# Two transformer layers on one core: weighted V copies kept per layer, a six-tile ring for the residual stream, and two score banks read by one VectorE instruction

## The chip, the cores and the metric

The kernel runs on one core of a Trainium2 chip. The metric is the device time of one execution in microseconds; lower is better. The kernel before takes 1658.69 us, the median of 3 runs (1657.44 to 1659.52). A core has five engines that run their own instruction streams and wait for each other through semaphores: TensorE (PE, matmuls into PSUM), ScalarE (ACT), VectorE (DVE), GpSimd (POOL) and SyncE (SP), which here issues all DMA transfers. PSUM has eight banks, each 128 partitions by 512 f32 numbers.

## The reference, cut to what matters

Four steps on x of shape [1, 2048, 512] in bf16: attention, MLP, attention, MLP, with the same weights in both rounds. The kernel calls the two attention steps layer 1 and layer 3.

```python
def _A_ref(x, wqkv, wo):            # attention, 32 heads of 16
    B, S, D = x.shape
    H = 32; Dh = D // H
    qkv = (x @ wqkv).reshape(B, S, 3, H, Dh).transpose(2, 0, 3, 1, 4)
    q, k, v = qkv[0], qkv[1], qkv[2]
    scores = jnp.einsum("bhqd,bhkd->bhqk", q, k) * Dh ** -0.5
    p = softmax(scores, axis=-1)
    o = jnp.einsum("bhqk,bhkd->bhqd", p, v)
    return o.transpose(0, 2, 1, 3).reshape(B, S, D) @ wo

def _B_ref(x, w1, b1, w2, b2):      # MLP, 512 -> 1376 -> 512
    y = layernorm(x)
    h = gelu(y @ w1 + b1)           # tanh form
    return h @ w2 + b2

x = A_x
x = x + _A_ref(layernorm(x), A_wqkv, A_wo)
x = x + _B_ref(layernorm(x), B_w1, B_b1, B_w2, B_b2)
x = x + _A_ref(layernorm(x), A_wqkv, A_wo)
x = x + _B_ref(layernorm(x), B_w1, B_b1, B_w2, B_b2)
```

## The kernel before

The Python program is a scheduler: it simulates the five engines with an estimated duration for every instruction, picks for each engine the ready task of lowest priority number, and writes out five fixed instruction streams. The durations in the code (0.66, 0.1 + 0.26e-3 * N and so on) are these estimates; on the chip only the order and the semaphore waits remain.

Attention goes by segments: one group of four heads (hg), one chunk of 512 queries (qc), 16 blocks of 128 keys (kb). A tile is one block of keys against 512 queries for one head (hp): a 128x512 matmul result in one PSUM bank. Most tiles are exponentiated by ScalarE, three and two banks in turn:

```python
            if self.wide:
                b0, G = ((0, 3), (3, 2))[gi % 2]
            ...
            S_.submit(Task("act", 1e-5 * gi, [I(lambda e, pt=pt, n=n, b0=b0: e.activation(out=self.PT[:, pt:pt + n, :], in_=self.ps[:, b0:b0 + n, :], func=ACTF.Exp, scale=EXPS), ...
```

Tiles of the key blocks DK = (3, 6, 9, 12, 15) may go to VectorE, which builds the bit pattern of the exponential by adding a constant to the scores and storing 16-bit integers. One such approximation is rough, so four of them are averaged, each shifted by a constant (SHIFT) and multiplied by a V that is scaled to match (WSHIFT). A tile on VectorE therefore costs one load from PSUM, shifts for k = 1, 2, 3 (two tiles in one instruction), and four matmuls with V instead of one:

```python
SHIFT = (0, 32, 64, 96)
WSHIFT = (1.0, 0.83984375, 0.70703125, 0.59375)
DK = (3, 6, 9, 12, 15)

    def d_load(self, d):                       # one score bank -> one half of dp[u]
        sg, j, b, bt, w = d
        ...
        self.S_.submit(Task("dve", 0.0, [I(lambda e: e.tensor_scalar(out=self.dp[:, u, w * 512:(w + 1) * 512], in0=self.ps[:, b, :], scalar1=BITS0, scalar2=None, op0=ALU.add), ...

    def job_d(self, bt):                       # the three shifts of a batch of two tiles
        for k in range(1, len(SHIFT)):
            v = yield ("get", "dp", sg["i"])
            pr = 0.15 if ... else 0.5 if self.left(sg) < DURGE else 2.5
            yield Task("dve", pr, [I(lambda e, k=k, v=v: e.tensor_scalar(out=self.dp[:, v, 0:N], in0=self.dp[:, u, 0:N], scalar1=float(SHIFT[k]), ...
```

Which tile goes where is decided while the program is written: `take_d` gives VectorE a tile only if one of two banks is free (the lane bank 5, or bank 7, MISCB, which projections and FFN also use), if VectorE is not behind, and if the scaled V is there. What is left over goes to ScalarE:

```python
    grp.append((sg, (sg["todo"] or sg["todod"]).pop(0)))      # ScalarE takes DK tiles when no others are left

    def take_d(self, hps):
        if ... self.dload > 1 or P.free["dve"] - S_.now > 1.3 or ... > DBACK:
            return None
        if not self.lane_busy and ("ret", DLANE) in S_.done and soon(DLANE):
            b = DLANE
        elif MISCB in mb.free and not mb.waiters and soon(MISCB):
            b = MISCB
        else:
            return None
        ...
        if not all(k in self.S_.done for k in [("qt", sg["i"])] + self.kv_keys(sg, kbs) + [("vs", sg["i"], kb) for kb in kbs]):
            return None
```

The scaled copies of V are made by GpSimd anew for every segment, three instructions each, into one of three slots:

```python
        self.vs = t("vs", [128, 3, 3, len(DK), 68], BF16)

    def job_vs(self, sg, i, kbs):
        q, hg, n = sg["qslot"], sg["hg"], len(kbs)
        src = self.V[:, hg, kbs[0]:kbs[-1] + 1:3, :, :].rearrange("p k h d -> p k (h d)")
        yield Task("pool", 0.8, [I(lambda e, k=k: e.tensor_scalar(out=self.vs[:, q, k - 1, i:i + n, :], in0=src, scalar1=WSHIFT[k], ...) for k in (1, 2, 3)])
```

Probabilities times V are summed in one PSUM bank (ACCB, bank 6), four heads side by side in the columns of the array. When a chunk of queries is done, the projection, layer norm and MLP of that chunk (`job_post`, `job_ffn`) run between the tiles of the next chunk; then its keys, values and queries for layer 3 are made. The residual stream is kept whole on the chip:

```python
        self.xres = t("xres", [128, NT, 512], BF16)           # NT = 16 tiles
        ...
            S_.submit(Task("dve", pr - 1, [I(lambda e, tt=tt, b=b: e.tensor_tensor(out=self.xres[:, tt, :], in0=self.ps[:, b, :], in1=self.xres[:, tt, :], op=ALU.add), ...
```

In gaps TensorE multiplies a zero tile (`fill_pe`)[...].

Of the kernel before, what the change touches and what calls it, by code (L numbers as in the profile page):

```python
# [8 lines left out]
BF16 = mybir.dt.bfloat16  # L9
# [4 lines left out]
ACTF = mybir.ActivationFunctionType  # L14
# [420 lines left out]
D_PRIO = 0.5  # L435
DBATCH = 2
DFLY = 4
# [3 lines left out]
ACCB = 6  # L441
MISCB = 7
DTAIL = 8
DURGE = 8
PV_NEAR = 0.7
PV_DEEP = 2
PV_COST = 0.5
PV_LEAST = 0.75
PV_IDLE = 0.25


class Builder:
# [44 lines left out]
    def alloc(self, es):  # L497
# [3 lines left out]
        self.xres = t("xres", [128, NT, 512], BF16)  # L501
# [27 lines left out]
        self.vs = t("vs", [128, 3, 3, len(DK), 68], BF16)  # L529
# [28 lines left out]
        self.q_scr = nc.dram_tensor("q_scr", [2, S, 1024], BF16, kind="Internal").ap()  # L558
        self.k_scr = nc.dram_tensor("k_scr", [S, 1024], BF16, kind="Internal").ap()
# [5 lines left out]
        pl["mb"] = Pool([7, 5, 4, 3, 2, 1, 0])  # L565
# [15 lines left out]
        pl["kmx"] = Pool(range(1))  # L581

# [39 lines left out]
    def build_startup(self):  # L622
# [5 lines left out]
        def ldx(a, b):  # L628
            n0("sp", I(lambda e: e.dma_start(self.xres[:, a:b, :], xr[:, a:b, :]), writes=[("x", tt) for tt in range(a, b)], dur=0.1))
# [9 lines left out]
        self.S_.when([("ks", 1, 1)], lambda: ldx(4, 8))  # L639
# [127 lines left out]
    def ln_group(self, tiles, slot, prio, eps1, eps0):  # L767

        for i, tt in enumerate(tiles):
            c = 4 * slot + i  # L770
            s = yield ("get", "st")
            yield Task("dve", prio, [I(lambda e, s=s, tt=tt: e.bn_stats(out=self.st[:, s, :], in_=self.xres[:, tt, :]), [("x", tt)], [("st", s)], 0.65)])
# [10 lines left out]
    def ln_apply(self, tt, slot, i, dst, dres, prio):  # L783
        c = 4 * slot + i
        return Task("dve", prio, [I(lambda e: e.tensor_scalar(out=dst, in0=self.xres[:, tt, :], scalar1=self.mv[:, c, 0:1], scalar2=self.rs[:, c:c + 1], op0=ALU.subtract, op1=ALU.mult),
                                    [("x", tt), ("mv", c), ("rs", slot)], [dres], 0.39)])
# [4 lines left out]
    def job_lnqkv(self, L, tiles, prio, later=None):  # L791
# [9 lines left out]
        if later is not None:  # L801
            yield ("keys", [("n2k", L, tt) for tt in range(self.NT)])
            for i, tt in enumerate(tiles):
                self.S_.spawn(self.job_qkv_tile(L, tt, slot, i, left, later + 0.01 * i, "q"), later + 0.01 * i)

    def job_qkv_tile(self, L, tt, slot, i, left, prio, what):
# [4 lines left out]
        yield self.ln_apply(tt, slot, i, xnr, RX, prio)  # L811
        left[0] -= 1
# [42 lines left out]
        if "v" in what:  # L855
# [3 lines left out]
            if direct:  # L859
# [3 lines left out]
                yield Task("dve", prio, [I(lambda e: e.tensor_copy(out=vdst, in_=psv), [("ps", b)], VR, 0.68)])  # L863
                S_.when([("ks", L, tt)], lambda: S_.mark(("kv", L, tt)))
# [849 lines left out]
```

## Time and profile before

The profile is one execution, recorded by the hardware profiler, with a span of 1661.8 us. What matters for the change:

| group (line of the kernel) | engine | instructions | busy us | mean ns |
|---|---|---|---|---|
| exponentials of score tiles, 1189 | ScalarE | 1321 | 1506.4 | 1259 with table loads |
| score matmuls, 1204 | TensorE | 4608 | 681.8 | 359 |
| loads of score tiles, 1281 | VectorE | 826 | 558.2 | 684 |
| shifts, 1312 | VectorE | 1257 | 488.8 | 431 |
| scaled V copies, 1065 | GpSimd | 240 | 238.5 | 995 |
| matmuls on a zero tile, 1114 | TensorE | 3792 | 182.0 | 277 |
| additions to the residual stream, 1469 and 1540 | VectorE | 60 | 40.9 | 682 |

Busy time counts each stretch in which a group has an instruction running once. The mean is of the single instructions; they overlap a little, so the mean times the count is more than the busy time. Matmuls overlap much more, and their ends are modelled, so a busy TensorE is not one at its limit. GpSimd's idle time before the scaled copies is 875.3 us. The mean traffic is 40 GB/s, and packets on the main DMA queue take 17.3% of the time of the 16 engines.

### The profile page before, as it was taken

The page shows a single profiled execution, that of the slowest core. Times are in us where ns is not written, and L with a number is a line of the kernel's source. Part 1 is how long each engine was busy: PE and PEld are TensorE (multiplying, and loading weights), DVE is VectorE, ACT ScalarE, POOL GpSimd, SP SyncE. Part 2 cuts the span into 40 slices and gives each one's busy share as a digit, 9 for nine tenths or more (in the row PEclk, how much of TensorE's full clock was granted, in tenths as well). Part 3 has the DMA queues.
Part 4 walks back from the last instruction along what each step waited for, and adds up shares of the span by engine and source line. Part 5 has one row for each costly group of instructions (what it writes and reads, how often), then busy time and mean ns, then how long its engine had stood idle before and what let it go on. Part 6 is the DMA issues. An engine that isn't in the chain of part 4 may idle for free.

```text
span 1661.8 us, 42068 instructions
## 1 busy us (share of the span) xinstructions
PE 1608.0 (97%) x17575; PEld 529.0 (32%) x17575; DVE 1452.7 (87%) x3146; ACT 1582.4 (95%) x1400; POOL 376.1 (23%) x575
## 2 busy tenths in 40 slices
PE   8999999999999999999999999999999999999998
PEld 5223322222222232222232323322232232344444
DVE  7789998888899898998989789999898969899893
ACT  4899999999999999999999999999999999999996
POOL 4345331111210112111121125511111111232220
PEclk9999999999999999999999999999999999899999
DMA  6562100202111121102362321000000000000000
GB/s 170 103 125 62 27 8 8 42 19 61 56 23 42 26 52 53 33 26 58 95 94 57 59 64 42 18 18 8 20 5 11 17 16 5 5 9 20 22 7 14
DMA packets 181243, 66.43 MB, mean 40 GB/s; under 512 B 160859, under 2 KB 175424, under 8 KB 181056
## 3 DMA queue, kind: packets, MB, share of 16 engines
q1 hardware_dynamic: 181056, 63.75, 17.3%
q8 instruction: 141, 2.31, 0.6%
q14 instruction: 46, 0.38, 0.1%
HBM read 19.96 MB, written 15.30 MB: 21 GB/s over the span
## 4 chain that ended last, share of the span: by engine, by line
PE 65%; ACT 27%; DVE 6%; issue 1%; DMA 1%; POOL 0%; POOLq 0%; SPq 0%; DVEq 0%
ACT PT L1189 25%; PE ps L1204 24%; PE ps L1373 19%; PE ps L840 5%; PE ps L1500 4%; PE ps L1538 4%; PE ps L1114 4%; PE ps L1467 3%; DVE dp L1281 2%; DVE dp L1312 2%; ACT h L1530 1%; PE ps L1117 1%; PE ps L953 1%; DMA xnT<-xn 0%; ACT L1189 0%
## 5 line engine op out<-in xcount | busy, mean ns | idle before, releaser
L1189 ACT ACTIVATE PT<-ps 128x1024 bf16<-128x1024 f32 (+1 forms) x1321 | 1506.4, 1259 | 49.5 <-PE ps L1204 43.1
L1204 PE MATMUL ps<-QT,KT 32*128 32x512 bf16 (+1 forms) x4608 | 681.8, 359 | 39.0 <-ACT PT L1189 16.9
L1281 DVE TENSOR_SCALAR dp<-ps 128x512 uint16<-128x512 f32 x826 | 558.2, 684 | 117.0 <-PE ps L1204 108.0
L1312 DVE TENSOR_SCALAR dp<-dp 128x1024 uint16<-128x1024 uint16 (+1 forms) x1257 | 488.8, 431 | 11.1 <-PE ps L1373 6.7
L1373 PE MATMUL ps<-PT,V 128*17 128x512 bf16 (+1 forms) x3672 | 486.7, 360 | 0.3 <-ACT PT L1189 0.3
L1065 POOL TENSOR_SCALAR vs<-V 128x340 bf16<-128x340 bf16 (+3 forms) x240 | 238.5, 995 | 875.3 <-PE ps L1373 851.0
L1373 PE MATMUL ps<-dp,vs 128*17 128x512 bf16 (+1 forms) x2808 | 420.7, 357 | 0.0
L1204 PEld LDWEIGHTS ps<-QT,KT 32*128 32x128 bf16 x4608 | 176.4, 91 | 568.3 <-issue 170.7
L1373 PE MATMUL ps<-dp,V 128*17 128x512 bf16 (+1 forms) x936 | 204.6, 359 | 2.7 <-DVE accT L1403 2.5
L1114 PE MATMUL ps<-wqkv,zw 128*32 128x256 bf16 x3792 | 182.0, 277 | 0.4 <-DVE dp L1281 0.4
L1373 PEld LDWEIGHTS ps<-PT,V 128*17 128x17 bf16 x3672 | 116.4, 88 | 119.4 <-issue 107.5
L1373 PEld LDWEIGHTS ps<-dp,vs 128*17 128x17 bf16 x2808 | 106.2, 89 | 113.6 <-issue 94.2
L1114 PEld LDWEIGHTS ps<-wqkv,zw 128*32 128x32 bf16 x3792 | 97.1, 96 | 67.1 <-issue 50.0
L1500 PE MATMUL ps<-yT,wf 128*128 128x512 bf16 (+3 forms) x396 | 101.7, 360 | 0.3 <-DVE dp L1281 0.3
L840 PE MATMUL ps<-wqkv,xnT 128*128 128x512 bf16 x336 | 96.1, 389 | 4.3 <-DMA xnT<-xn 3.4
L1403 DVE STREAM_TRANSPOSE accT<-ps 128x512 f32<-128x512 f32 (+1 forms) x88 | 58.0, 659 | 13.7 <-PE ps L1373 12.7
L1467 PE MATMUL ps<-wo,OT 128*128 128x512 bf16 x240 | 67.2, 383 | 0.0
L1373 PEld LDWEIGHTS ps<-dp,V 128*17 128x17 bf16 x936 | 50.5, 89 | 48.1 <-issue 26.7
L1524 DVE TENSOR_SCALAR h<-ps,b1c 128x512 bf16<-128x512 f32 (+2 forms) x88 | 61.9, 704 | 3.6 <-PE ps L1500 2.9
L1443 DVE STREAM_TRANSPOSE OT<-ob 128x512 bf16<-128x512 bf16 (+1 forms) x72 | 46.0, 638 | 0.2
L1500 PEld LDWEIGHTS ps<-yT,wf 128*128 128x128 bf16 (+1 forms) x396 | 28.1, 99 | 54.2 <-issue 26.9
L1538 PE MATMUL ps<-wf,h 128*128 128x512 bf16 x160 | 44.9, 383 | 0.1
(171 smaller groups left out, 794.7 us busy)
## 6 DMA issues: line engine op xcount, KB each, us to landing
wf<-in_B_w_dram SPq DMA_DIRECT2D x90, 128.0 KB, 2.6
q_scr<-qk SPq DMA_DIRECT2D x22, 256.0 KB, 2.0
k_scr<-qk SPq DMA_DIRECT2D x12, 256.0 KB, 2.1
out_dram<-xres SPq DMA_DIRECT2D x16, 128.0 KB, 1.7
v_scr<-vst SPq DMA_DIRECT2D x12, 136.0 KB, 1.7
V<-v_scr SPq DMA_DIRECT2D x8, 204.0 KB, 4.7
wqkv<-in_A_wqkv_dram SPq DMA_DIRECT2D x3, 512.0 KB, 3.9
q_scr<-h SPq DMA_DIRECT2D x6, 256.0 KB, 3.6
```

The source lines that it names most:

```text
L840: yield Task("pe", prio, [I(lambda e, c=c: e.matmul(self.ps[:, b, :], lhsT=xnT[:, c, :], rhs=self.wqkv[:, c, which * 512:which * 512 + 512 ...
L1065: yield Task("pool", 0.8, [I(lambda e, k=k: e.tensor_scalar(out=self.vs[:, q, k - 1, i:i + n, :], in0=src, scalar1=WSHIFT[k], scalar2=None ...
L1114: P.op("pe", lambda e, p=p: e.matmul(self.ps[p:p + 32, b, 0:w], lhsT=self.zw[:, 0:32], rhs=rhs[:, 0:w], start=st, stop=st, skip_group_chec ...
L1189: S_.submit(Task("act", 1e-5 * gi, [I(lambda e, pt=pt, n=n, b0=b0: e.activation(out=self.PT[:, pt:pt + n, :], in_=self.ps[:, b0:b0 + n, :] ...
L1204: return [I(lambda e, kb=kb, i=i: e.matmul(self.ps[:, b, i * W:(i + 1) * W], lhsT=self.KT[32 * hp:32 * hp + 32, hg, kb * 128:(kb + 1) * 12 ...
L1281: self.S_.submit(Task("dve", 0.0, [I(lambda e: e.tensor_scalar(out=self.dp[:, u, w * 512:(w + 1) * 512], in0=self.ps[:, b, :], scalar1=BIT ...
L1312: yield Task("dve", pr, [I(lambda e, k=k, v=v: e.tensor_scalar(out=self.dp[:, v, 0:N], in0=self.dp[:, u, 0:N], scalar1=float(SHIFT[k]), sc ...
L1373: ops.append((i, I(lambda e, hp=hp, v=v, ap=ap[:, i * W:(i + 1) * W], first=first and i == 0, W=W: e.matmul(self.ps[32 * hp:32 * hp + 17, ...
L1467: yield Task("pe", pr, [I(lambda e, hg=hg, i=i, b=b: e.matmul(self.ps[:, b, :], lhsT=self.OT[:, hg, i * 128:(i + 1) * 128], rhs=self.wo[:, ...
L1500: yield Task("pe", pr, [I(lambda e, c=c: e.matmul(self.ps[0:M, b, off:off + W], lhsT=self.w1(fc, c), rhs=self.yT[:, c, 0:W], start=(c == 0 ...
L1524: S_.submit(Task("dve", pr - 0.7, [I(lambda e, fc=fc, M=M, b=b: e.tensor_scalar(out=hv[0:M, fc * W:(fc + 1) * W], in0=self.ps[0:M, b, 0:W] ...
L1538: yield Task("pe", pr, [I(lambda e, fc=fc, i=i, b=b: e.matmul(self.ps[:, b, :], lhsT=self.gt(fc, i, W), rhs=self.w2(L, fc), start=(fc == 0 ...
```

## The change

The change has three parts and a new set of constants.

First, the scaled copies of V are made once per layer for all head groups and kept; a tile on VectorE then no longer waits for a copy of its segment. The copies need 8 slots instead of 3.

Second, to make room for them, the residual stream is no longer kept whole. Six tiles stay in a ring; the others are stored to DRAM (`x_scr`) and loaded again when they are needed: for the late query pass of layer 1 from the input, for the residual addition after each attention from the input or from `x_scr`. At the start tiles 6 to 15 of x lie where the copies will be.

Third, when a second score bank is given to VectorE before the load of the first has been written out, the two loads become one instruction that reads both banks. A first load now has a lower priority (D_FIRST), to give the second time to come. Banks 6 and 7 change places, so that the two score banks are 5 and 6.

```diff
-D_PRIO = 0.5
+D_PRIO = 0.4
+NXR = 6
+XAHEAD = 4
+D_FIRST = 1.2
-ACCB = 6
-MISCB = 7
-DTAIL = 8
-DURGE = 8
-PV_NEAR = 0.7
+ACCB = 7
+MISCB = 6
+DTAIL = 10
+DURGE = 6
+PV_NEAR = 0.5
-PV_COST = 0.5
-PV_LEAST = 0.75
-PV_IDLE = 0.25
+PV_COST = 0.6
+PV_LEAST = 0.8
+PV_IDLE = 0.3
...
-        self.xres = t("xres", [128, NT, 512], BF16)
+        self.xres = t("xres", [128, NXR, 512], BF16)
-        self.vs = t("vs", [128, 3, 3, len(DK), 68], BF16)
+        self.vs = t("vs", [128, 8, 3, len(DK), 68], BF16)
+        self.x_scr = nc.dram_tensor("x_scr", [S, 512], BF16, kind="Internal").ap()
...
+    def job_xload(self, L, why, tiles, prio):
+        for tt in tiles:
+            k = yield ("get", "xr", prio)
+            self.xslot[tt] = k
+            src = (self.A_x[0] if L == 1 else self.x_scr)[tt * 128:(tt + 1) * 128, :]
+            yield self.dma(lambda e, k=k, src=src: e.dma_start(self.xres[:, k, :], src), [("xscr", tt)] if L == 3 else [], [("x", k)], prio, 0.45)
+            self.S_.mark(("xl", L, why, tt))
...
-        if sg["dks"] and not (L == 1 and sg["nparts"] == 2 and part == 0):
-            self.S_.spawn(self.job_vs(sg, 0, sg["dks"]), 0.8)
-    def job_vs(self, sg, i, kbs): ...
+    def weigh(self, hgs, kbs, after=()):          # three GpSimd instructions, k = 1, 2, 3
+    def job_weigh(self, L, kb):                   # layer 1 blocks, and blocks 12 and 15 of layer 3: all 8 groups at once
+        xe = range(NXR, 16) if L == 1 else ()
+        yield ("keys", [("xe", k) for k in xe])
+        yield from self.weigh(range(8), [kb], [("x", k) for k in xe])
+        self.S_.mark(("vw", L, kb))
     def job_kload(self, hg):                      # layer 3: V of blocks 0 to 11 comes from DRAM by group
...
+        yield from self.weigh([hg], [kb for kb in DK if kb < 12])
+        self.S_.mark(("vwl", hg))
...
     def d_load(self, d):
-        self.S_.submit(Task("dve", 0.0, [I(lambda e: e.tensor_scalar(out=self.dp[:, u, w * 512:(w + 1) * 512], in0=self.ps[:, b, :], scalar1=BITS0, ...
+        pend = self.S_.pend["dve"]
+        ds = [d]
+        if "wait" in bt and bt["wait"][0] in pend:
+            pend.remove(bt["wait"][0])
+            ds = [bt["wait"][1], d]
...
+        b0, b1 = ds[0][2], ds[-1][2]
+        src = self.ps[:, b0:b1 + 1:max(b1 - b0, 1), :]
+        t = Task("dve", 0.0 if n > 1 or w else D_FIRST, [I(lambda e: e.tensor_scalar(out=self.dp[:, u, w * 512:(w + n) * 512].rearrange("p (k w) -> p k w", k=n), in0=src, scalar1=BITS0, ..., 0.127 + 0.533 * n)])
...
     def job_post(self, L, qc):
+        yield ("keys", [("ot", L, qc, XAHEAD)])
+        S_.spawn(self.job_xload(L, "r", tiles, 1.4), 1.4)
         yield ("keys", [("ot", L, qc, hg) for hg in range(8)])
...
     def x_done(self, L, tt, b, pr):
-        if L == 3:
-            ... store the tile to the output
+        dst = (self.out[0] if L == 3 else self.x_scr)[tt * 128:(tt + 1) * 128, :]
+        S_.submit(self.dma(lambda e: e.dma_start(dst, x), [RX], ...), cb=lambda: S_.mark(("xst", L, tt)))
+        S_.when([("xst", L, tt)] + ([("xn3", tt)] if L == 1 else []), lambda: self.xfree(tt))
```

Lines of three dots and shortened argument lists are cuts. Not shown are the places that only look up in which slot a tile of the residual stream lies, and a shorter priority number (1.05 for 1.6) for the work after the third chunk of layer 1.

## The prediction

> **What bounds the kernel now.** I read the page's table of busy time first, then the slices of the span, then the groups by shape, and last single stretches of the timeline. The table of busy time says that three engines are nearly full, so it decides nothing by itself:
>
> ```profile
> PE 1608.0 (97%) x17575; PEld 529.0 (32%) x17575; DVE 1452.7 (87%) x3146; ACT 1582.4 (95%) x1400; POOL 376.1 (23%) x575
> ...
> PE 65%; ACT 27%; DVE 6%; issue 1%; DMA 1%; POOL 0%; POOLq 0%; SPq 0%; DVEq 0%
> ```
>
> The second of these lines heads the chain of waits; with PE and ACT at 65% and 27% it points at the loop in which scores go from TensorE to ScalarE. Busy time by stretch separates the engines (columns: stretch, its length, busy time of PE, weight loads, DVE, ACT, POOL with counts, granted clock, DMA share, GB/s):
>
> ```profile
> 0.00:100.00 100.00, 91.94 (x797) 38.65 (x797) 73.11 (x166) 71.56 (x82) 40.99 (x87) 0.97 0.59 128
> ...
> 500.00:700.00 200.00, 195.33 (x1875) 54.87 (x1871) 178.93 (x380) 196.76 (x169) 34.66 (x48) 1.00 0.16 41
> ...
> 1200.00:1400.00 200.00, 194.92 (x2125) 58.62 (x2126) 176.23 (x376) 197.32 (x171) 30.55 (x29) 1.00 0.05 12
> ```
>
> In the steady stretches ScalarE is busy 98.4% and 98.7% of the time; VectorE has about 10% left. TensorE looks equally full, but not all of what it does is needed: the page's group for line 1114, matmuls on a zero tile[...], is 182.0 us. I therefore take ScalarE as the bound, TensorE as nearly one, and VectorE as the engine that decides how much ScalarE must do. That last point is in the groups:
>
> ```profile
> L1189 ACT ACTIVATE PT<-ps 128x1536 bf16<-128x1536 f32 x628 | 931.0, 1483 | 29.6 <-PE ps L1204 23.7
> L1189 ACT ACTIVATE PT<-ps 128x1024 bf16<-128x1024 f32 x693 | 727.5, 1057 | 19.9 <-PE ps L1204 19.3
> ...
> L1281 DVE TENSOR_SCALAR dp<-ps 128x512 uint16<-128x512 f32 x826 | 558.2, 684 | 117.0 <-PE ps L1204 108.0
> L1312 DVE TENSOR_SCALAR dp<-dp 128x1024 uint16<-128x1024 uint16 x1221 | 479.8, 434 | 11.0 <-PE ps L1373 6.7 <-DVE xres L1469 0.3
> ```
>
> A score tile is 128x512. ScalarE exponentiates 628*3 + 693*2 = 3270 of them, VectorE takes 826 (the loads on line 1281), together 4096. The code lets VectorE take at most the key blocks of DK, some 1200 tiles, and hands what it does not get to in time to ScalarE. So the split floats: whatever makes VectorE cheaper per tile moves tiles off ScalarE. ScalarE's price is 1506.4 us (page, line 1189) / 3270 = 0.461 us a tile. VectorE's is (558.2 + 488.8) / 826 = 1.27 us a tile, the second number being line 1312 on the page.
>
> The whole span then closes as a sum: ScalarE idle 1661.8 - 1582.4 = 79 us, other ScalarE work 1582.4 - 1506.4 = 76 us, and 0.461 * 3270 = 1507 us. One more tile on VectorE is worth 0.46 us as long as the other engines follow.
>
> The last lines are timelines of VectorE and GpSimd around the making of weighted V copies:
>
> ```profile
> 563.04 1.10 DVE L1312 TENSOR_SCALAR dp<-dp 128x1024 uint16<-128x1024 uint16 x3
> ...
> 567.60 3.38 POOL L1065 TENSOR_SCALAR vs<-V 128x340 bf16<-128x340 bf16 x3 [24.53 <-PE ps L1373]
> 567.66 1.88 DVE L1312 TENSOR_SCALAR dp<-dp 128x1024 uint16<-128x1024 uint16 x3
> ```
>
> The same three shifts take 1.10 us with GpSimd idle and 1.88 us while it multiplies V.
>
> [...]Over all shifts, instruction by instruction and counting only time that no earlier VectorE instruction covers, I get 341 ns for 1007 shifts with GpSimd idle, 441 ns for 99 fully under a GpSimd instruction, 411 ns for 151 partly. A load from PSUM shows no such difference[...] (644 against 623 ns).
>
> [...]
>
> [...]the ScalarE row above with 1.48 us for three banks against 1.06 for two shows the same kind of fixed cost (0.43 a bank, about 0.2 an instruction).
>
> **The change part by part.**
> 1. Weighted V copies. Removed: 240 GpSimd instructions, 238.5 us. Added: in layer 1 five blocks x 3 weights over all eight head groups (544 elements a row), in layer 3 eight groups x 3 (272 elements) and blocks 12 and 15 x 3 (544). From the groups by shape (340 elements 1091 ns, 136 elements 624 ns) the slope is 2.3 ns an element, so 544 elements are about 1.56 us. 21 * 1.56 + 24 * 0.92 = 55 us. GpSimd is on no critical path (0% of the chain), so the 184 us removed are worth only what they did to VectorE: 99 * 0.10 + 151 * 0.07 = 20 us of slower shifts, of which I count three quarters, 15 us of VectorE time.
> 2. Ring of six tiles. This pays for the memory of part 1. It adds about 60 transfers of 128 KB: 12 reloads for the late query pass, 32 for the residual additions, 16 stores. DMA is at 17.3% now and such a transfer lands in 1.7 to 3.0 us; reloads start four head groups ahead, about 90 us. I count 0. One new order: copies of layer 1 lie where tiles 6 to 15 start out, so none can be made until all of them are normalised. Before, the first VectorE tile is at 99 us, and the last V block of that layer is cast at 93.4 us; two blocks of copies (2 * 3 * 1.56 = 9 us) then come before the first is usable. At worst 10 us later, at 19 tiles in the stretch from 100 to 150 us, that is 4 tiles, 2 us lost.
> 3. Pairs. The two banks are the lane bank 5 and bank 6, and bank 6 is also the only bank for projections and FFN in this phase. A pair forms only if the second score is issued before VectorE has started on the first. In the trace the loads are a median 1.6 us apart and only 135 follow directly on another load. The lower priority of a first load and the other constants push towards pairs, so I take 40% of about 860 tiles, 170 pairs; at 0.13 us each[...] that is 22 us of VectorE.
> 4. Constants (when P times V is batched, when shifts turn urgent). They are set for the new arrangement; I count 3 us gained, a guess.
>
> Sum: VectorE is freed of 15 + 22 = 37 us. At a new price of 1.27 - 0.04 = 1.23 us a tile that is 30 more tiles, 856 in all, and 30 * 0.461 = 14 us less ScalarE. TensorE pays 90 more column matmuls, four abreast at about 0.21 us, 5 us, which fit into the 182 us of filler. 14 - 2 + 3 = 15 us, and a little for fewer waits where the written schedule assumed shifts without the GpSimd collision: 17 us. 1658.7 - 17 = 1642.
>
> **The rivals.**
> - The tiles do not move: VectorE's 117 us of idle time before loads is waiting for scores, so a faster VectorE waits longer. For it: that row. Against it: VectorE is at 89% in the steady stretches with queueing in between. Time: 1655 to 1660.
> - Pairs hold both banks for 1.2 us, first loads are put back, projections wait for bank 6, and the handover from layer 1 to layer 3 (VectorE 82% in 900 to 1000 us, the weakest stretch) gets longer. Time: 1665 to 1685.
> - Pairing is the rule rather than the exception (80%) and shorter shifts bring the score loop into step: 340 pairs * 0.13 + 15 = 59 us, 50 tiles, 23 us, and some of the 79 us of ScalarE idle with it. Time: 1620 to 1630.
> - The ring stalls: four tiles of one chunk hold their slots until their keys are made, so the next chunk finds two free slots. The first chunk's tiles come free near 420 us and the next residual is due near 450, so I expect no wait; if there is one, 5 to 15 us per layer.
>
> **Range and chances.** Part 1 is nearly sure, part 3 uncertain by a factor of two, and the written order of all instructions changes, which can move a kernel this full by 10 us either way. I predict 1642 us, 8 in 10 between 1620 and 1661. Faster by over 2% means under 1625.5, which needs the third rival: 0.18. Slower by over 2% means over 1692: 0.03. Within 2%: 0.79.
>
> **What would show it.** Right: GpSimd's group for the copies near 55 us and 45 instructions; shifts at about 0.41 us instead of 0.43; a 128x1024 load from two banks at about 1.2 us, some 170 of them; 850 to 870 tiles on VectorE and ScalarE's line near 1490 us; ScalarE still 98% busy in the steady stretches. Wrong: loads still 826 or fewer; ScalarE idle well over 79 us; new waits of VectorE on a transfer into xres; or shifts as slow as before with GpSimd silent.

## The result, and the profile after

The changed kernel takes 1671.97 us (median of 4 runs, 1665.36 to 1674.12) against 1658.81: a ratio of 1.0074, 95% interval 1.0045 to 1.0103. It is slower by three quarters of a per cent, where 1% faster was predicted. The span of the profiled execution grew from 1661.8 to 1672.3 us.

First the page of the changed kernel: busy time by engine, the granted TensorE clock in 40 slices, and the head of the chain of waits.

```profile
PE 1589.1 (95%) x17721; PEld 541.8 (32%) x17846; DVE 1422.3 (85%) x3043; ACT 1583.5 (95%) x1402; POOL 189.3 (11%) x380
...
PEclk9989999999999999999999999999988999999999
...
PE 59%; ACT 31%; DVE 6%; issue 2%; DMA 1%; POOL 0%; POOLq 0%; SPq 0%; DVEq 0%
```

GpSimd lost 187 us and VectorE 30 us of work, as the change intends. ScalarE has as much as before (1583.5 against 1582.4), so its idle time grew from 79.4 to 88.8 us (span less busy time). The new marks are in the second line: slice 3 at the start and two slices late in the span, in which the clock is down. Busy time by stretch (PE, weight loads, DVE, ACT, POOL, clock, DMA share, GB/s):

```profile
0.00:100.00 100.00, 90.47 (x826) 39.44 (x833) 73.03 (x165) 70.91 (x81) 54.80 (x94) 0.97 0.64 138
500.00:700.00 200.00, 191.59 (x1934) 56.77 (x1948) 175.04 (x375) 195.73 (x168) 8.64 (x24) 1.00 0.18 45
1200.00:1400.00 200.00, 192.20 (x1931) 56.08 (x1938) 168.23 (x350) 188.17 (x162) 1.35 (x2) 0.94 0.06 14
```

Between 500 and 700 us ScalarE is about as busy as before. In the last of these stretches, which had 197.32 us before, it is 9 us short, and the clock is 0.94 instead of 1.00. The groups by shape for the parts of the change:

```profile
L1243 ACT ACTIVATE PT<-ps 128x1536 bf16<-128x1536 f32 x629 | 932.1, 1482 | 41.6 <-PE ps L1258 36.7
L1243 ACT ACTIVATE PT<-ps 128x1024 bf16<-128x1024 f32 x693 | 726.8, 1056 | 17.6 <-PE ps L1258 17.2
...
L1379 DVE TENSOR_SCALAR dp<-dp 128x1024 uint16<-128x1024 uint16 x1218 | 466.6, 423 | 14.0 <-PE ps L1440 9.8
L1347 DVE TENSOR_SCALAR dp<-ps 128x512 uint16<-128x512 f32 x642 | 437.2, 685 | 120.9 <-PE ps L1258 114.6
L1347 DVE TENSOR_SCALAR dp<-ps 128x1024 uint16<-128x1024 f32 x90 | 109.7, 1219 | 17.4 <-PE ps L1258 16.2
...
L1112 POOL TENSOR_SCALAR vs<-V 128x544 bf16<-128x544 bf16 x21 | 34.7, 1651 | 19.9 <-DVE V L901 13.9 <-DVE xn L794 4.7
L1112 POOL TENSOR_SCALAR vs<-V 128x204 bf16<-128x204 bf16 x24 | 19.7, 830 | 14.8 <-DMA V<-v_scr 13.8
```

VectorE has 642 + 2 * 90 = 822 tiles, four fewer than before; the two ScalarE rows hardly changed. A pair costs 1219 ns against 2 * 685. VectorE's idle time before loads, nearly all of it waiting for scores, went from 117.0 to 138.3 us. Most of what VectorE was freed of has turned into waiting.

Where the time went is in ScalarE's busy time by stage (stage, its length, busy time, clock, DMA share, GB/s). Before:

```profile
28.00:110.00 82.00, 71.47 (x73) 0.96 0.57 108
...
800.00:1060.00 260.00, 250.20 (x222) 1.00 0.32 65
1060.00:1430.00 370.00, 364.17 (x314) 1.00 0.05 12
```

And after:

```profile
28.00:110.00 82.00, 68.39 (x70) 0.91 0.61 119
...
800.00:1060.00 260.00, 252.55 (x225) 0.99 0.32 69
1060.00:1430.00 370.00, 354.23 (x305) 0.96 0.06 15
```

3 us are lost at the start and 10 us in layer 3; the stages from 110 to 1060 and from 1430 to 1620 us together give 3 us back. Both losses are where the clock is lower. A mean clock of 0.986 over 1672.3 us is 2 * 0.014 * 1672.3 = 47 us at half clock, the only lower value (0.5) that the trace's clock record has; 0.994 over 1661.8 us is 20 us. The trace's own record of the clock has 47.8 us after (6.8 us at 38, 10.2 at 103, 3.4 at 1052 and at 1099, 13.7 at 1209, 10.2 at 1256) and 20.5 us before (6.8 at 38, 3.4 at 1400, 10.2 at 1434), the last microseconds after the final matmul left out. Every stretch is one or more windows of 3.4 us.

A timeline of one such window of the changed kernel, 1252 to 1256 us, just before the stretch at 1256 (start, duration, engine; in brackets idle time and what ended it):

```profile
1252.64 1.23 DVE L1347 TENSOR_SCALAR dp<-ps 128x1024 uint16<-128x1024 f32 x1
...
1253.92 0.32 PEld L1258 LDWEIGHTS ps<-QT,KT 32*128 32x128 bf16 x5 [0.62 <-DVE dp L1347]
1253.92 0.81 PE L1258 MATMUL ps<-QT,KT 32*128 32x512 bf16 x5
...
1254.78 1.22 DVE L1347 TENSOR_SCALAR dp<-ps 128x1024 uint16<-128x1024 f32 x1
...
1255.13 0.39 PE L1258 MATMUL ps<-QT,KT 32*128 32x512 bf16 x2
...
1256.48 0.61 PE L1258 MATMUL ps<-QT,KT 32*128 32x512 bf16 x3 [0.95 <-ACT PT L1243]
```

TensorE waits 0.62 us for a pair to be read and later 0.95 us for ScalarE, with no zero matmuls in between; what it does meanwhile uses a quarter of the array or less per instruction (32 rows for scores, 17 columns for P times V). Counted by an estimate, each such matmul as a quarter of the 0.213 us that the program assumes for 512 columns (full-array matmuls back to back start 215 ns apart in both traces at full clock, 400 to 430 at half), the window ahead of each half-clock stretch in both traces is filled to under 0.39. A thin window isn't enough, though: by the same count 2 of some 14 such windows in the kernel before and 5 of some 15 in the changed kernel were followed by half clock. Here the waits (0.62 and 0.95 us) and the quarter-filled array come together, on a row that is busy 95% of the time over the span; which of them brings the clock down, if either does, is not separated by any run.

### The profile page after: what moved, and what is told of

The parts are those of the page before. It is cut to its first block, busy times and chain, and to the rows that moved or that the text cites. A ratio compares the mean times of both kernels' runs of the same rounds, so it can differ in the third digit from the quotient of the medians.

```text
span 1672.3 us, 42273 instructions
## 1 busy us (share of the span) xinstructions
PE 1589.1 (95%) x17721; PEld 541.8 (32%) x17846; DVE 1422.3 (85%) x3043; ACT 1583.5 (95%) x1402; POOL 189.3 (11%) x380
## 4 chain that ended last, share of the span: by engine, by line
PE 59%; ACT 31%; DVE 6%; issue 2%; DMA 1%; POOL 0%; POOLq 0%; SPq 0%; DVEq 0%
ACT PT L1243 27%; PE ps L1258 23%; PE ps L1440 17%; PE ps L1167 5%; PE ps L878 4%; PE ps L1573 4%; PE ps L1611 3%; DVE dp L1347 3%; PE ps L1538 3%; ACT h L1603 2%; DVE dp L1379 2%; PE ps L1170 1%; PE ps L994 1%; ACT L1243 1%; ACT L1603 1%
## 5 line engine op out<-in xcount | busy, mean ns | idle before, releaser
L1243 ACT ACTIVATE PT<-ps 128x1024 bf16<-128x1024 f32 (+1 forms) x1323 | 1507.4, 1258 | 59.2 <-PE ps L1258 53.9
L1347 DVE TENSOR_SCALAR dp<-ps 128x512 uint16<-128x512 f32 (+1 forms) x732 | 547.0, 751 | 138.3 <-PE ps L1258 130.8
L1379 DVE TENSOR_SCALAR dp<-dp 128x1024 uint16<-128x1024 uint16 (+1 forms) x1248 | 473.9, 421 | 14.0 <-PE ps L1440 9.8
L1440 PE MATMUL ps<-dp,V 128*17 128x512 bf16 (+1 forms) x930 | 199.4, 362 | 0.4 <-DVE accT L1470 0.2
L1167 PE MATMUL ps<-wqkv,zw 128*32 128x256 bf16 x4088 | 192.9, 280 | 0.3 <-DVE dp L1347 0.2
L1167 PEld LDWEIGHTS ps<-wqkv,zw 128*32 128x32 bf16 x4088 | 104.5, 97 | 76.0 <-issue 49.1
L1573 PE MATMUL ps<-yT,wf 128*128 128x512 bf16 (+3 forms) x363 | 93.3, 357 | 6.1 <-issue 3.7
L878 PE MATMUL ps<-wqkv,xnT 128*128 128x512 bf16 x302 | 87.0, 390 | 9.1 <-issue 3.7
L1538 PE MATMUL ps<-wo,OT 128*128 128x512 bf16 x217 | 62.5, 388 | 4.3 <-issue 2.9
L1112 POOL TENSOR_SCALAR vs<-V 128x204 bf16<-128x204 bf16 (+1 forms) x45 | 54.3, 1213 | 34.8 <-DVE V L901 13.9
```

The source lines that it names most:

```text
L878: yield Task("pe", prio, [I(lambda e, c=c: e.matmul(self.ps[:, b, :], lhsT=xnT[:, c, :], rhs=self.wqkv[:, c, which * 512:which * 512 + 512 ...
L1112: return [Task("pool", 0.8, [I(lambda e, k=k: e.tensor_scalar(out=dst[k - 1], in0=src, scalar1=WSHIFT[k], scalar2=None, op0=ALU.mult), [(" ...
L1167: P.op("pe", lambda e, p=p: e.matmul(self.ps[p:p + 32, b, 0:w], lhsT=self.zw[:, 0:32], rhs=rhs[:, 0:w], start=st, stop=st, skip_group_chec ...
L1347: t = Task("dve", 0.0 if n > 1 or w else D_FIRST, [I(lambda e: e.tensor_scalar(out=self.dp[:, u, w * 512:(w + n) * 512].rearrange("p (k w) ...
L1440: ops.append((i, I(lambda e, hp=hp, v=v, ap=ap[:, i * W:(i + 1) * W], first=first and i == 0, W=W: e.matmul(self.ps[32 * hp:32 * hp + 17, ...
L1538: yield Task("pe", pr, [I(lambda e, hg=hg, i=i, b=b: e.matmul(self.ps[:, b, :], lhsT=self.OT[:, hg, i * 128:(i + 1) * 128], rhs=self.wo[:, ...
```

## The experiments

Two theories stood at first. One: the change moved no tiles, and the loss is half clock. Other: pairs, or GpSimd's instructions, hold somebody up. All ratios are to the kernel before, run on the same chip, where it took 1661 to 1663 us; times of experiments on different chips are best compared by these ratios.

**1 and 2, zero matmuls in all gaps.** The order of all other instructions is kept; wherever the code already looks for a gap for zero matmuls it fills the whole gap.

```diff
+FILL_MORE = 9.0
+        more = min(room, int((FILL_MORE - P.activity(end)) * 3.41 / FILL_T + 0.999), 80) - max(n, 0)
```

> The changed kernel with every other instruction in the same order, but 135 more groups of zero matmuls (256 columns each) in the gaps that TensorE has anyway. Clock theory: the changed kernel loses its time in the 41 us after the start in which TensorE runs at half clock (13.7 us before the change), so with more filler the half-clock time falls below 15 us and the time to 1660 to 1664 us. Rival (the pairs make TensorE wait, the clock only follows): the gaps stay, half clock stays near 40 us and the time at 1670 to 1674 us.

> The kernel before, same order, with 127 more groups of zero matmuls by the same rule: a control. Clock theory: it has only 13.7 us of half clock to lose, so at most 4 us faster, 1655 to 1659 us. If filler itself costs time, it is slower than 1659 us.

After 1668.92 (1.0037 [1.0022, 1.0052]), before 1664.5 (1.0022 [1.0010, 1.0035]). In the profiled executions the half-clock time went from 47.8 to 41.0 us and from 20.5 to 17.1: the gaps that the code knows of are mostly not the thin windows. Where one stretch did vanish, the 6.8 us at 38, the changed kernel gained 4 us at that place.

The single runs test the clock theory better than these medians. In the 22 runs of experiment 1, one program with one order, the mean clock goes from 0.998 to 0.982 (7 to 60 us at half clock) and the time from 1657.7 to 1678.6 us; a straight line through them has 0.37 us for each us at half clock. In 43 runs of the kernel before on the same chip the clock goes from 1.000 to 0.988, the time from 1654.2 to 1672.2 us, and the line has 0.40. So the order of the changed kernel is nearly as fast as the kernel before whenever the clock stays up, and the half clock of one order differs from run to run. Which of the two causes the other the lines don't say; experiments 3 and 5 do, place by place.

**3, pairs issued as two loads.** Same order, same waits; each pair is two instructions of one bank each, one after the other.

```diff
-        [I(lambda e: e.tensor_scalar(out=self.dp[:, u, w * 512:(w + n) * 512]..., in0=src, scalar1=BITS0, ...
+        [I(lambda e: [e.tensor_scalar(out=self.dp[:, u, x[4] * 512:(x[4] + 1) * 512], in0=self.ps[:, x[2], :], scalar1=BITS0, ...) for x in ds][-1],
```

> The changed kernel, same order and same waits, but each of the 90 paired loads is issued as two single loads. VectorE gets 90 times 0.11 to 0.15 us, 10 to 14 us, more to do. If what VectorE saves were worth anything by itself in a written order, the time rises by 5 to 14 us over 1672 us; if the order fixes everything and VectorE has room, by less than 3 us.

1669.33 us, 1.0049 [1.0030, 1.0069]. VectorE's busy time rose by only 5.6 us (1422.3 to 1427.9), so this is all that pairs save. The kernel got no slower. In it the stretch at 1209 is missing. Busy time by stretch, first the changed kernel:

```profile
1200.00:1250.00 50.00, 47.48 (x483) 13.06 (x479) 42.60 (x90) 44.76 (x40) 0.00 (x0) 0.86 0.03 7
1250.00:1300.00 50.00, 47.77 (x498) 14.67 (x497) 38.72 (x84) 44.67 (x40) 1.35 (x2) 0.90 0.09 17
```

Then the one with split pairs:

```profile
1200.00:1250.00 50.00, 46.58 (x535) 14.17 (x531) 47.94 (x109) 49.38 (x45) 0.00 (x0) 1.00 0.03 7
1250.00:1300.00 50.00, 48.50 (x496) 14.48 (x495) 38.92 (x90) 44.73 (x39) 1.35 (x2) 0.90 0.11 17
```

With the clock at 1.00 ScalarE does 45 instructions instead of 40 in the same 50 us, in the same order of instructions. Beside it, where both kernels have 0.90, they are alike. Instruction by instruction the split kernel gains 5.5 us at 1203 to 1223 us and nothing of that size elsewhere: 5.5 / 13.7 = 0.40 us of time for each us at half clock, as in the lines of single runs above.

**4, GpSimd kept busy in the changed kernel.** Same order, with 240 multiplications of V into a spare tile where the kernel before made its copies.

```diff
+            for kk in (1, 2, 3):
+                self.S_.submit(Task("pool", 0.8, [I(lambda e, kk=kk: e.tensor_scalar(out=jdst, in0=vsrc, scalar1=WSHIFT[kk], ..., op0=ALU.mult), ..., 0.0)]))
```

> The changed kernel, same order on all other engines, but GpSimd again multiplies V for every segment, 240 instructions of up to 340 elements, into a scratch tile that nobody reads. This puts the removed collisions back, about 20 us on VectorE's shifts by the working in the prediction. If removing them was worth its full size, the time rises by 10 to 20 us over 1672 us; if it was worth little because the split of tiles is fixed, by 0 to 4 us.

1702.79 us, 1.0249 [1.0227, 1.0272], far more than expected of a collision. Shifts went from 421 to 450 ns, but the multiplications may also delay GpSimd's other work, of which the order knows nothing (not measured), and half-clock time rises to 68.3 us (17.1 of it at 654). About 8 of the 31 us are half clock by the price of experiment 3; the rest isn't settled. The run is no measure of the collision alone; experiment 7 is.

**5 and 6, the clock forced up.** Same orders, with about 325 groups of four zero matmuls put ahead of score matmuls wherever the array had been under half full by the program's count.

```diff
+        n = min(int((BOOST - P.activity(P.drain)) * 3.41 / FILL_T + 0.999), BOOST_CAP)   # BOOST = 0.5
+        for i in range(n): ... e.matmul(self.ps[p:p + 32, ACCB, 0:FILL_N], lhsT=self.zw[:, 0:32], ...)
```

> The changed kernel, all other instructions in the same order, with 326 more groups of zero matmuls placed in front of score matmuls wherever the work issued in the last 3.4 us fills less than half of the array, whether there is a gap or not. The earlier filler run left half clock at 43 us and so did not test the clock. Clock theory (a microsecond of half clock costs about 0.4 us, as the split run shows, where 13.7 us less came with 5.3 us less): if half clock falls from 41 to about 10 us, the time falls by 10 to 12 us to 1659 to 1662 us, less what the filler itself costs. Rival (the order has gaps of its own): the clock stays up and the time stays above 1668 us.

> The kernel before with the same rule, 324 groups. Clock theory: it has 13.7 to 18.7 us of half clock to lose, so 3 to 6 us faster at most, 1655 to 1659 us, and the gap between the two kernels closes to within 4 us. If the filler costs its own 0.11 us a group on the path, it is slower by up to 10 us.

After 1682.48 (1.0119 [1.0092, 1.0145]), before 1681.05 (1.0108 [1.0084, 1.0132]), with 17.1 and 6.8 us at half clock where 47.8 and 20.5 were without them. The forced matmuls cost more than they save and are no remedy. But where they removed the stretches at 1209 and 1256 (13.7 and 10.2 us), instruction by instruction the changed kernel gained 4.7 and 3.5 us. And with the clock up in both, the two kernels differ by 0.1%: nothing else of the change shows, within some 0.4% by these intervals and with the forced matmuls in both.

**7, collisions taken away in the kernel before.** Same order; the 240 copies write one column of each 68 (most of the copies then stay at the zero that a memset at the start writes, so the output is another).

```diff
-  e.tensor_scalar(out=self.vs[:, q, k - 1, i:i + n, :], in0=src, ...
+  e.tensor_scalar(out=self.vs[:, q, k - 1, i:i + n, 0:1], in0=src[:, :, 0:1], ...
```

> The kernel before, same order and same waits, but the scaled copies of V are 5 elements instead of 340 in a row (the output is then not the reference's: four of five copies are left at zero). This is the first part of the change alone, on the old order. If removing the GpSimd collisions is worth what putting them back cost in the changed kernel (31 us), the time falls to 1625 to 1640 us and the loss of the change must come from its new order. If the collisions are worth little at a fixed split of tiles, 1655 to 1661 us.

1660.72 us, 0.9997 [0.9981, 1.0013]. The groups of VectorE on its page:

```profile
L1282 DVE TENSOR_SCALAR dp<-ps 128x512 uint16<-128x512 f32 x826 | 560.1, 686 | 129.8 <-PE ps L1205 119.4
L1313 DVE TENSOR_SCALAR dp<-dp 128x1024 uint16<-128x1024 uint16 (+1 forms) x1257 | 472.5, 419 | 10.3 <-PE ps L1374 6.0
```

VectorE is freed of 19.5 us (1452.7 to 1433.2), 16 of it in the shifts, and waits 13 us longer before its loads (129.8 against 117.0). The time stays. This is the first part of the change by itself, and the point at which the prediction breaks.

**8, the changed kernel without pairs.** The order is written anew: 819 tiles.

```diff
-D_FIRST = 1.2
+D_FIRST = 0.0
...
-        if "wait" in bt and bt["wait"][0] in pend:
+        if False:
```

> The changed kernel without pairs: every load reads one bank at once, and the order of everything is written anew (819 tiles on VectorE instead of 822). Rival theory (pairs hold two banks and let TensorE wait, which costs the clock): half clock falls below 20 us and the time to 1658 to 1664 us. Clock and order theory: the pairs are not the cause, the time stays within 1664 to 1680 us, as any new order may have its half-clock stretches elsewhere.

1664.81 us, 1.0021 [1.0007, 1.0035], with 17.1 us at half clock: better than with pairs by about half a per cent, but with another order, and 1664.8 us lies at the edge of both expectations, so pairs as such aren't convicted.

**9, 10 and 12, the durations that the order is written from.** The order of all instructions, and with it the split of tiles, is computed when the program is written, with an assumed duration for each instruction. Only these are altered.

```diff
-  ... 0.127 + 0.533 * n)])          # a load of n banks; 9: 0.09 + 0.533 * n    10: 0.2 + 0.56 * n    12: 0.66 -> 0.62
-  ... 0.1 + 0.26e-3 * N)])          # a shift            9: 0.06 + 0.26e-3 * N  10: 0.15 + 0.26e-3 * N   12: as 9
```

> The changed kernel with only the two durations lowered by which its written plan hands tiles to VectorE: a load 0.127 -> 0.09 us + 0.533 per bank, a shift 0.1 -> 0.06 us + its elements. No instruction is made cheaper; the plan, written anew, gives VectorE 862 tiles instead of 822 and forms 98 pairs instead of 90. Theory (the split is fixed when the program is written, from these durations, so a cheaper VectorE moves nothing by itself, and the ScalarE price of a tile is real once it does move): ScalarE's exponentials fall by 40 x 0.46 = 18 us to about 1489, and the time falls below the changed kernel by 8 to 18 us (1654 to 1664), with the half-clock time of TensorE of the new order moving it by 0.37 us each (a guess of the order: less of it than the 49 us of the changed kernel). Rival (VectorE has no time to spare when it counts, the 30 us freed lie in waits for scores): ScalarE's line falls as well, but its idle time rises by as much, loads are late, and the time stays at 1668 to 1680.

> The opposite: written durations raised to 0.20 + 0.56 per bank for a load and 0.15 + elements for a shift; the plan gives VectorE 774 tiles, 77 pairs. Theory: ScalarE's exponentials rise by 48 x 0.46 = 22 us to about 1529 and the time rises to 1685 to 1700. Rival (VectorE's lateness is what costs): ScalarE's line rises but its idle time falls below 80 us, and the time stays within 1665 to 1680.

> The kernel before with the same two written durations lowered by the same amounts (load 0.66 -> 0.62, shift 0.1 -> 0.06 + elements): 859 tiles instead of 826, nothing else. Its shifts do collide with GpSimd, so VectorE really needs more than is written. Theory (the freed VectorE time of the change is what makes extra tiles payable): VectorE is late here, ScalarE's exponentials fall to about 1491 but the time stays at 1654 to 1668, above the first kernel of this set by 3 us or more. Rival (the split alone counts, VectorE has slack in both): 1640 to 1652, the change isn't needed for it.

Measured: 1673.07 (1.0073 [1.0052, 1.0094]), 1687.4 (1.0150 [1.0128, 1.0171]) and 1675.13 us (1.0073 [1.0048, 1.0099]). ScalarE's group on the page of experiment 9:

```profile
L1243 ACT ACTIVATE PT<-ps 128x1024 bf16<-128x1024 f32 (+1 forms) x1307 | 1489.1, 1260 | 70.7 <-PE ps L1258 66.2
```

VectorE's loads of it, by shape:

```profile
L1347 DVE TENSOR_SCALAR dp<-ps 128x512 uint16<-128x512 f32 x666 | 451.3, 683 | 96.7 <-PE ps L1258 90.1
L1347 DVE TENSOR_SCALAR dp<-ps 128x1024 uint16<-128x1024 f32 x98 | 119.4, 1218 | 9.8 <-PE ps L1258 8.9
```

666 + 2 * 98 = 862 tiles: the written durations are the lever, with 774 tiles in experiment 10 and 859 in 12. ScalarE's line follows, 1489.1 and 1524.0 us against 1507.4, 0.46 us for each of the 40 tiles moved in 9 and 0.35 for each of the 48 in 10. But in 9 ScalarE's idle time rose from 88.8 to 102.8 us, which gives back 14 of the 18 in the profiled execution (by the median all), and in 12 from 79.4 to 96.4, more than the 13 us that its exponentials fell by. On the tiles and on the time of 10 the theory held, on the time of 9 the rival; 12 is slower than either of its expectations. Over its six runs 12 has a median of 57 us at half clock, some 40 more than the kernel before, which at 0.40 is 16 us and covers its loss; its extra tiles then bring in a few us at most.

**11, the written durations near the measured ones, and five constants set anew.** Load 0.107 + 0.533 a bank, shift 0.075 + elements.

```diff
-FILL_ACT = 0.62    +FILL_ACT = 0.66
-DTAIL = 10         +DTAIL = 9
-DURGE = 6          +DURGE = 8
-PV_NEAR = 0.5      +PV_NEAR = 0.45
-PV_IDLE = 0.3      +PV_IDLE = 0.25
```

The set was picked among many by the end that the written order itself computes, so its order is the best of many.

> The changed kernel with the written durations brought to about what the traces show as new time of an instruction (load 0.107 + 0.533 per bank, shift 0.075 + elements) and six constants of the plan set anew (when shifts turn urgent, when P times V is batched, how much filler): 853 tiles, 101 pairs. Theory: ScalarE's exponentials about 1493; the time 1645 to 1658, below both kernels. Rival: 1665 to 1675, the plan's gain is lost to lateness that it doesn't know of.

1643.33 us (1641.60 to 1646.61), 0.9890 [0.9872, 0.9909]: faster than both kernels. Its page:

```profile
PE 1569.0 (95%) x16899; PEld 524.0 (32%) x17030; DVE 1448.1 (88%) x3102; ACT 1566.4 (95%) x1389; POOL 189.4 (12%) x380
...
L1243 ACT ACTIVATE PT<-ps 128x1024 bf16<-128x1024 f32 (+1 forms) x1310 | 1490.5, 1262 | 47.2 <-PE ps L1258 42.3
...
L1347 DVE TENSOR_SCALAR dp<-ps 128x512 uint16<-128x512 f32 (+1 forms) x752 | 565.2, 756 | 101.9 <-PE ps L1258 94.4
```

853 tiles, ScalarE's line at 1490.5 and its idle time at 76.7 us. That is what the prediction had summed up to (856 tiles, 1492 us, 1642 us), but it took another written order to get there, and experiment 17 shows how much of it is that order's luck.

**13 to 18, is it the change or the order?** 13 puts the durations and constants of 11 on the kernel before; 14 is 11 without pairs (D_FIRST kept at 1.2); 15, 16, 17 and 18 shift one constant of the kernels after, before, 11 and 13 slightly.

```diff
15  -PV_NEAR = 0.5     +PV_NEAR = 0.52
16  -FILL_ACT = 0.62   +FILL_ACT = 0.63
17, 18  -PV_NEAR = 0.45    +PV_NEAR = 0.47
```

> The kernel before with exactly the written durations and constants of e11 (load 0.64, shift 0.075 + elements, the same six constants): 843 tiles on VectorE instead of 826. Its copies of V are still made 240 times and it has no pairs. Theory (the change frees VectorE time, and this time is worth something once the plan uses it): ScalarE's exponentials about 1498.5, the time 1650 to 1660, 7 us or more above e11. Rival (the numbers of the plan make the whole difference, and the change is worth nothing): 1640 to 1647, like e11's 1643.

> e11 without pairs, everything else as there: copies once per layer, 839 tiles, all loads single. Theory (pairs are what makes the 853 tiles payable): 1650 to 1658. Rival (pairs are worth nothing, the plan is): 1641 to 1647.

> The changed kernel with one constant of the plan shifted slightly (a P times V matmul may be planned 0.52 us instead of 0.50 ahead of its data), which writes the order anew: 830 tiles, 102 pairs, and by the plan 15 us instead of 27 us of windows in which TensorE's array is less than a third full. Theory (what made the changed kernel slower is the half-clock time of its particular order): half-clock time below 30 us and time 1658 to 1667, about that of the kernel before. Rival (pairs or late waits slow it): 1669 to 1675 again.

> The kernel before with one constant shifted slightly (filler up to 0.63 of the array instead of 0.62): 835 tiles, by the plan 27 us of windows less than a third full instead of 19. Theory (the order of the kernel before is a lucky one among its neighbours): 1668 to 1682, half-clock time 35 us or more. Rival (the arrangement of before is better in itself): 1656 to 1664.

> e11 with one constant shifted slightly (0.45 -> 0.47 us, how far ahead a P times V matmul may be planned), which writes its order anew: 851 tiles, 98 pairs. Theory (e11's gain over e13 belongs to the change): 1643 to 1650. Rival (most of it is the luck of one order, picked out of many): 1651 to 1660.

> e13 with the same shift (0.45 -> 0.47 us): 842 tiles. Theory: 1653 to 1660 as e13 (1656), above e17 by 5 us or more. Rival: within 4 us of e17.

All orders side by side. Time is the median, idle is the span less ScalarE's busy time, half clock is from the trace's record; these two, the exponentials and the tiles are of the profiled execution. The last column is the median over all runs, worked out from each run's mean clock (to about 2 us; for the kernel before from the runs beside the experiments).

| kernel | tiles on VectorE | time us | ratio to before | exponentials us | ScalarE idle us | half clock us | half clock us, all runs |
|---|---|---|---|---|---|---|---|
| before | 826 | 1658.8 | 1 | 1506.4 | 79.4 | 20.5 | 13 to 18 |
| after | 822 | 1672.0 | 1.0074 [1.0045, 1.0103] | 1507.4 | 88.8 | 47.8 | 47 |
| 3 after, pairs split | 822 | 1669.3 | 1.0049 [1.0030, 1.0069] | 1506.3 | 84.5 | 34.1 | 35 |
| 8 after, no pairs | 819 | 1664.8 | 1.0021 [1.0007, 1.0035] | 1506.3 | 79.5 | 17.1 | 25 |
| 9 after, lower durations | 862 | 1673.1 | 1.0073 [1.0052, 1.0094] | 1489.1 | 102.8 | 44.4 | 50 |
| 10 after, higher durations | 774 | 1687.4 | 1.0150 [1.0128, 1.0171] | 1524.0 | 82.1 | 13.7 | 22 |
| 12 before, lower durations | 859 | 1675.1 | 1.0073 [1.0048, 1.0099] | 1493.6 | 96.4 | 44.4 | 57 |
| 11 after, anew | 853 | 1643.3 | 0.9890 [0.9872, 0.9909] | 1490.5 | 76.7 | 27.3 | 23 |
| 13 before, anew | 843 | 1656.4 | 0.9965 [0.9950, 0.9979] | 1496.5 | 83.9 | 20.5 | 20 |
| 14 as 11, no pairs | 839 | 1652.3 | 0.9931 [0.9908, 0.9953] | 1496.3 | 77.3 | 13.7 | 23 |
| 15 after, shifted | 830 | 1660.2 | 0.9981 [0.9967, 0.9995] | 1502.3 | 80.6 | 23.9 | 20 |
| 16 before, shifted | 835 | 1676.6 | 1.0080 [1.0059, 1.0100] | 1500.1 | 94.8 | 13.7 | 22 |
| 17 as 11, shifted | 851 | 1662.8 | 1.0017 [1.0001, 1.0032] | 1494.2 | 90.7 | 47.8 | 46 |
| 18 as 13, shifted | 842 | 1656.8 | 0.9975 [0.9967, 0.9984] | 1498.6 | 84.0 | 23.9 | 17 |

What follows. Experiment 15 has 102 pairs, more than the changed kernel's 90, and in its trace none of the half-clock stretches after 120 us:

```profile
PEclk9979999999999999999999999999999999999999
```

It is as fast as the kernel before. So pairs do not slow the kernel; one order of it does. Experiment 13 against 11 looked like 12 us for the change (by the ratios), and 14 like 7 of these for the pairs. But 17, two hundredths of a microsecond beside 11 in one constant, has 851 tiles and pairs too and needs 1662.8 us (1654.9 to 1676.9 over 22 runs): the trace has 47.8 us at half clock, and the longest stretch, 13.7 us at 1041, is in the page's clock line as the second 8, slice 26 of 40 (the first, slice 3, is the start, as in the changed kernel):

```profile
PEclk9989999999999999999999999899999999999999
```

It is slower even than the rival expected: what 11 gained over 13 is in large part the luck of one order picked out of many. Experiment 18, put at 5 us or more above 17 or within 4 us of it, came out 6 us below. At 0.40 us each, the half clock of the medians makes some 9 of the 20 us between 11 and 17; the rest is the order. Five orders of the kernel before (before, 12, 13, 16, 18) have a mean ratio of 1.0019, five of the changed one with pairs (after, 9, 11, 15, 17) 1.0007, and with experiment 10, the sixth, 1.0031; each set spreads over 1% to 3%. A worth of the change between these can't be told from nothing.

In 16 the theory gave the right time for a wrong reason: its half-clock time is 13.7 us, not over 35. The busy times of the stage 800 to 1060 us, in which layer 1 hands over to layer 3:

```profile
800.00:1060.00 260.00, 245.22 (x2751) 80.94 (x2750) 222.18 (x480) 233.37 (x207) 68.49 (x134) 0.99 0.33 67
```

ScalarE has 233.37 us there, 17 us less than the 250.20 of the kernel before, at a clock of 0.99. An order can lose as much by a stage that drains.

## Why the prediction was wrong

**The step that failed** is "So the split floats: whatever makes VectorE cheaper per tile moves tiles off ScalarE." It was read out of the code as if VectorE took its next tile when it is free. In fact the split is fixed when the order is written, from assumed durations (0.66 us a load, 0.1 us plus elements a shift) in which the collision with GpSimd (a shift added 441 ns of new time fully under a GpSimd instruction, 341 with GpSimd idle) never was. A cheaper VectorE then only waits longer: 19.5 us freed and 0.9997 in experiment 7, 30 us freed and 822 tiles instead of 856 in the changed kernel. The saving of pairs, unlike the collision, is in the assumed durations (1.193 us a pair against 2 * 0.66), and still the order has four tiles fewer; with the constants of experiment 11 pairs bring 14 tiles (853 against 839 in 14), so why they bring none here stays open. The 14 us of the sum became 0 (ScalarE's line rose by 1.0 us). The rival "the tiles do not move" named this row of waits as its sign and was right about it; its 1655 to 1660 us is what the measured time comes to without the 11 to 13 us of half clock below.

**The second step that failed** is "One more tile on VectorE is worth 0.46 us as long as the other engines follow." For ScalarE's busy time it is right (0.46 in experiment 9). For the time it can't be counted on: 9 and 12 moved 40 and 33 tiles, and neither is faster than the kernel it started from.

**Part 1** was right in its size: 15 to 20 us of VectorE time expected, 16 measured in the shifts and 19.5 in all (experiment 7); 45 copies in 34.7 + 19.7 = 54.4 us, expected 55. An instruction of 544 elements took 1651 ns, not 1560, and the layer 3 ones have 204 elements, not 272. The prediction took the timeline near 567 us as shifts slowed by GpSimd's copies. Instruction by instruction it reads:

```profile
567.60 1.06 POOL L1065 TENSOR_SCALAR vs<-V 128x340 bf16<-128x340 bf16 x1 [24.53 <-PE ps L1373]
567.66 0.69 DVE L1312 TENSOR_SCALAR dp<-dp 128x1024 uint16<-128x1024 uint16 x1
```

The shift started 0.06 us after the multiplication and ended 0.3 us before it; 57 shifts lie so inside one multiplication, with a mean of 532 ns, against 414 ns for the shifts of this trace that overlap no GpSimd instruction. By the trace, in which GpSimd's times are rough, these shifts were slowed and not held until the multiplication ended. By what, no run shows.

**Part 2** was right: no wait for a reloaded tile stands out among the groups, and DMA stays at 1% of the chain. The late start was put at 2 us; ScalarE has 3.1 us less in 28 to 110 us. Part of it is half clock at 103 us, which the kernel before doesn't have.

**Part 3** was right in the price, 2 * 685 - 1219 = 151 ns of busy time where 0.13 us was counted (the author's estimate, not shown by the trace of before), and wrong in the count: 90 pairs, 22% of the tiles, not 170. It saved little: 5.6 us of VectorE's busy time in all by experiment 3, against 22.

**The loss** was in no term of the sum. In the two traces 27.3 us more at half clock at 0.40 is 11 us, and the spans differ by 10.5. By the medians, 47 us against 13 to 18 us come to 11 to 13 us, and the times differ by 13.2. The single runs and experiments 3 and 5 stand behind it, and 15, in which another order of the same kernel has no such stretch in layer 3. The rival with 1665 to 1685 us had the size, but not the cause: it put the loss on the handover from layer 1 to layer 3, which in fact is 2 us better (252.55 against 250.20 us of ScalarE), and on held banks, which the split pairs of experiment 3 hold as long.

**The range** counted the written order as 10 us either way. That was about the right size (16: 1676.6 us after a shift of one constant by 0.01; 17: 1.3% above 11), but it was laid around a gain that wasn't there: around no gain it would have been 1649 to 1669, with the 1672 measured just outside.

What stays open: what brings the clock down after one thin window and not after another; why the extra tiles of experiments 9 and 12 came with 14 and 17 us more idle time in their traces, of which half clock explains none in 9 and 9 to 10 us in 12; and whether a choice among as many orders of the kernel before would reach 1643 us too, which was not tried.

## What to carry to other kernels

When the order of instructions is written ahead of time, a cheaper instruction need not change anything until the assumed duration changes (19.5 us freed, ratio 0.9997 in experiment 7), and then the whole order does: look for where the split of work is decided before giving a freed microsecond a price. Compare a change to such a kernel with several orders of both versions, because one order against one order measures mostly the luck of the two; here two orders that differ in one constant lie 1.3% apart, and the two kernels 0.7%. And read the clock line by slices, and the mean clock of every run beside its time: here a TensorE that was 95% busy, much of it with matmuls on a quarter of the array, spent 47.8 us at half clock, and not in every run alike (7 to 60 us over the runs of experiment 1).

## What the runs showed that was not expected

- Half clock came with TensorE busy 97% of the span before and 95% after, behind windows of 3.4 us in which its matmuls, by the estimate that counts each by the share of the array that it uses, filled less than 0.39; most windows as thin were not followed by it (12 of some 14 before, 10 of some 15 after). In one and the same order 13.7 us of it cost 5.5 us, and single runs of one program give 0.37 to 0.40 us for each us.
- Zero matmuls where TensorE is needed cost more than they save: with about 325 groups the kernel before was 1.1% slower and the changed kernel 0.5%, while half-clock time fell by 14 and 31 us.
- One VectorE instruction over two banks took 1219 ns against 1370 for two; split into single loads, only 62 of these 151 ns came back as busy time (5.6 us for 90 pairs).
